# Attention with normalised queries and keys: shifts moved from VectorE and GpSimd to accumulating transfers, and a retuned plan with fewer wide QK matmuls

## The chip, the cores and the metric

The kernel runs on one core of a Trainium2 chip. The metric is the device time of one execution in microseconds (us), a median over several executions. A profile shows a single execution, so its span differs a little from the median, and it leaves out about 2 us at the ends.

Engines in the profile's lines: PE is TensorE's matmul, PEld its weight load, DVE is VectorE, ACT is ScalarE, POOL is GpSimd, SP is SyncE. An engine name with a "q" is that engine's queue of transfer issues.

## The reference

One batch, 32 heads, 2048 positions, head dimension 20, bf16 inputs:

```python
qn = q / (sqrt((q*q).sum(-1, keepdims=True)) + 1e-6)
kn = k / (sqrt((k*k).sum(-1, keepdims=True)) + 1e-6)
logits = einsum('bhqd,bhkd->bhqk', qn, kn) * t[None, :, None, None]
return einsum('bhqk,bhkd->bhqd', softmax(logits), v)
```

The work is dominated by the exponential of 32 x 2048 x 2048 logits, which are 2048 units of 128 rows by 512 columns. In the profile below ScalarE takes 0.453 us for one (650.0 us / 1436 units), so alone it would need 928 us. The kernel shares the exponential between two engines.

## The kernel before

**ScalarE's share.** TensorE writes QK products into PSUM (`psA`), ScalarE takes the exponential two or three units of 512 columns at a time into `p_ring`, and TensorE multiplies these with the values (PV).

**VectorE's share, the "tiles".** A tile is 2048 columns of products in `psD`. VectorE converts it in two instructions of 1024 columns to 16-bit integers, `x*1024*log2(e) + constant`, whose bits are then read as fp16. This is a piecewise linear exponential. To smooth it, TensorE multiplies four versions of the tile with the values: the tile itself and three copies with 256, 512 or 768 added to the integer, each with values scaled down by 2^(-added/1024). The added constants (shifts) are what the change is about:

```python
PHASES = (256, 512, 768)
NX, NE = 4, 3                    # rings: converted tiles, shifted copies
DVE_TILES = [4, 4, 4, 5, ...]    # tiles of each head; 153 in all
KDN = (3, 3, 3, ...)             # tiles of each head whose third shift is GpSimd's
# ... (in add_dgroup: one tile; x is its converted form xt[sx])
for i in range(len(PHASES)):
    dst, war = ss[i][se], t1s + old(f"s{i}", NE)
    if i < 2 or jg < 2 or js[0] - d0[...] >= KDN[...]:
        sh.append([dv(f"s{i}.", lambda e, tk, i=i, dst=dst: e.tensor_scalar(
            dst[:, 0:w], x, float(PHASES[i]), None, ALU.add), 0.533, war)])
        continue
    sh.append([])
    for c in range(0, w // 2, PCH):          # GpSimd, in two halves
        u = add("POOL", f"s{i}.{js[0]}.{c}", lambda e, tk, ...: e.tensor_tensor(...ALU.add), ...)
```

**Preparing a head.** Queries and keys are loaded (`qk_sb`), normalised (`qkn`, on GpSimd), and transposed by a DMA transpose into `qkT`, a ring of three. Ten small transfers, four `qz` and six `kR` (the rotations, below), then copy the transposed rows into four arrangements, which lets four QK matmuls of 32 rows run side by side. SyncE issues them all, in order.

**The plan.** Nothing decides an order on the chip. While the kernel is built, a list scheduler (class `Program`) simulates the engines with an assumed duration for each instruction and an assumed landing time for each transfer (`lat`: 4.5 us for loads of q and k, 3.0 for values, 3.0 for a transpose), and fixes the order of every engine's queue. On the chip each queue runs strictly in that order with semaphore waits. If something lands later than planned, whatever stands behind its waiter in the same queue stops too. (A transfer has landed when its completion is signalled.)

**Wide QK.** The kernel can run a QK matmul over 32, 64 or 128 rows with the same result, the extra rows being zeros. The planner makes matmuls wide where TensorE's load in 3.41 us would otherwise be below a threshold (`LOAD`), so as to hold up its clock.

Of the kernel before, what the change touches and what calls it, by code (L numbers as in the profile page):

```python
# [12 lines left out]
I32 = mybir.dt.int32  # L13
I16 = mybir.dt.int16
# [29 lines left out]
class Program:  # L44
# [5 lines left out]
    SWITCH = 0.25  # L50
# [3 lines left out]
    PASSES = 10  # L54
# [3 lines left out]
    SPARE = 0.0  # L58
    DSL = 0.8
    HOLDA = 9.0  # L60
    HPE = 0.1
    HOLD = {"DVE": 0.0, "PE": HPE}
# [10 lines left out]
    def schedule(self):  # L73


        heavy = set()
        choice = [t for t in self.tasks if t.modes]
        for _ in range(self.PASSES):
            for t in choice:
                tag, t.rows, t.dur, t.work = t.modes[t in heavy]  # L80
                t.name = tag + t.name[2:]
            self.list_schedule()
            pe = [t for t in self.order["PE"] if t.end > self.LIGHT]
            more, i, load = set(), 0, 0.0
            work = [t.work for t in pe]
            for j, t in enumerate(pe):
                while pe[i].end < t.end - self.TICK:
                    load -= work[i]
                    i += 1
                for tier in range(3):  # L90
                    m = j - 1
                    while i and load < self.LOAD and m >= i:
                        u = pe[m]
                        if u.modes and u not in heavy and u not in more and (
                                tier == 2 or u.modes[1][2] == u.dur or tier == 1 and
                                u.modes[1][2] - u.dur <= min(v.start for v in u.users) - u.end - 0.2 - self.SPARE):
                            more.add(u)
                            work[m] += u.modes[1][3] - u.work
                            load += u.modes[1][3] - u.work
                        m -= 1  # L100
                load += work[j]
            if not more:
                break
            heavy |= more
        self.heavy = heavy
        for t in self.tasks:
            if t.trig is not None:
                t.deps.append(t.trig)
        return self.order

    def list_schedule(self):
# [49 lines left out]
        def pool_fill(now):  # L161

            n = 0
            while True:
# [21 lines left out]
                heapq.heappush(events, (t.end, 1, t.seq, t))  # L186
# [135 lines left out]
def bass_standalone__qk_norm__prompt_kernel(  # L322
# [20 lines left out]
    NX = 4  # L343
# [7 lines left out]
    SPREAD = 1.0  # L351
# [5 lines left out]
    DVE_TILES = [4, 4, 4, 5, 5, 5, 5, 5, 4, 5, 5, 5, 5, 5, 4, 5, 5, 5, 5, 5, 4, 5, 5, 5, 5, 5, 4, 5, 5, 5, 5, 5]  # L357
# [7 lines left out]
    KDN = (3, 3, 3, 3, 3, 3, 3, 3, 3, 3, 3, 3, 3, 3, 3, 2, 3, 3, 3, 3, 3, 3, 3, 3, 3, 4, 3, 3, 3, 4, 2, 3)  # L365
# [3 lines left out]
    with ExitStack() as es:  # L369
# [7 lines left out]
        two = sbuf("two", [128, 1], I32)  # L377
        ident = sbuf("ident", [128, 128], BF16)
# [27 lines left out]
        def memset(eng, ap, val, dur, pri):  # L406
            return add(eng, "z", lambda e, tk: e.memset(ap, val), dur, pri=pri)
# [35 lines left out]
        memset("POOL", two[:, :].bitcast(I16), PHASES[2], 0.1, -98)  # L443
# [331 lines left out]
        def add_dgroup(jg):  # L775
# [35 lines left out]
            sh = []  # L811
            for i in range(len(PHASES)):
                dst, war = ss[i][se], t1s + old(f"s{i}", NE)
                if i < 2 or jg < 2 or js[0] - d0[D_tiles[js[0]][0]] >= KDN[D_tiles[js[0]][0] % len(KDN)]:
                    sh.append([dv(f"s{i}.", lambda e, tk, i=i, dst=dst: e.tensor_scalar(  # L815
                        dst[:, 0:w], x, float(PHASES[i]), None, ALU.add), 0.533, war)])
                    continue
                sh.append([])
                for c in range(0, w // 2, PCH):
                    n = min(PCH, w // 2 - c)  # L820
                    u = add("POOL", f"s{i}.{js[0]}.{c}", lambda e, tk, i=i, dst=dst, c=c, n=n: e.tensor_tensor(  # L821
                        dst[:, 2 * c:2 * (c + n)].bitcast(I32), xt[sx][:, 2 * c:2 * (c + n)].bitcast(I32),
                        bass.AP(two, 0, [two[:, :].ap[0], [0, n]]), ALU.add), 0.25 + n * PRATE, war, due + SHP)
                    u.win = 0.02 + n * PRATE
                    sh[-1].append(u)
            dusers["x", jg] = [u for us in sh for u in us]
            for nm, tile, dep, ph in [("x", xt[sx], t1s, None)] + [(f"s{i}", ss[i][se], sh[i], i) for i in range(len(PHASES))]:
                us = dusers.setdefault((nm, jg), [])
                for i, j in enumerate(js):
                    h, rg = D_tiles[j]  # L830
                    p = add("PE", f"pv{nm}{j}", lambda e, tk, h=h, rg=rg, i=i, tile=tile, ph=ph: pv_mm(
                        e, h, lambda g: rg[g],
                        lambda g: tile[:, 2048 * i + 512 * GORD[g]:2048 * i + 512 * GORD[g] + 512].bitcast(FP16), ph),
                        PE_MM, dep + pv_base(h) + (vsc[h] if ph is not None else []), due + 0.2)
                    pv_users[h].append(p)
                    us.append(p)
# [76 lines left out]
```

## Time and profile before

Four executions: median 667.70 us (667.33 to 667.84).

| | before |
|---|---|
| span of the profiled execution | 665.3 us |
| ScalarE busy / VectorE busy | 657.1 (99%) / 654.2 (98%) |
| TensorE / GpSimd busy | 601.3 (90%) / 355.3 (53%) |
| granted TensorE clock | 0.999 |
| DMA | 36.24 MB, queue q1 34.5% of the engines' time |

These are lines of the page of the kernel before: busy times, clock in 40 slices, DMA queue, the chain of waits that ended last by engine, and three groups. A group line has line, engine, operation, tiles and shapes, count, then busy us and mean ns of one, then the engine's idle time just before such instructions and what ended most of it.

```profile
PE 601.3 (90%) x5914; PEld 166.3 (25%) x5959; DVE 654.2 (98%) x927; ACT 657.1 (99%) x584; POOL 355.3 (53%) x364
PEclk9999999999999999999999999999999999999999
q1 hardware_dynamic: 196512, 35.22, 34.5%
ACT 90%; DVE 5%; DMA 1%; SPq 1%; PE 1%; POOL 0%; issue 0%; ACTq 0%
L757 ACT ACTIVATE p_ring<-psA 128x1024 bf16<-128x1024 f32 (+1 forms) x575 | 650.0, 1371 | 2.8 <-PE psA L666 2.7
L803 DVE TENSOR_SCALAR xt<-psD 128x1024 int16<-128x1024 f32 x306 | 371.1, 1213 | 4.4 <-PE psD L666 3.3
L815 DVE TENSOR_SCALAR ss<-xt 128x2048 int16<-128x2048 int16 x365 | 241.8, 683 | 0.9
```

The two exponential engines are both full; in 650 us of exp, ScalarE waited 2.8 us. A quicker kernel therefore needs less work on both. VectorE's shifts, 241.8 us, are the natural thing to give away.

### The profile page before, as it was taken

How to read it: one execution, taken by the hardware profiler on the slowest of the kernel's cores; microseconds unless marked ns; L12 is line 12 of the kernel's file. 1: busy time of each engine (PE TensorE's matmuls, PEld its weight loads, DVE VectorE, ACT ScalarE, POOL GpSimd, SP SyncE). 2: the span in 40 equal slices, each digit the busy share in tenths (PEclk: the TensorE clock that was granted, in tenths of full speed). 3: DMA queues.
4: the chain of work that ended last, by engine and by line, in shares of the span. 5: the costliest groups of instructions: out<-in, count | busy, mean ns of one | idle time of the engine just before them, and what ended most of it. 6: DMA issues, size and time to landing. Idle time of an engine off the chain costs nothing.

```text
span 665.3 us, 14541 instructions
## 1 busy us (share of the span) xinstructions
PE 601.3 (90%) x5914; PEld 166.3 (25%) x5959; DVE 654.2 (98%) x927; ACT 657.1 (99%) x584; POOL 355.3 (53%) x364
## 2 busy tenths in 40 slices
PE   7798989989889999898999999999899989999987
PEld 2222222222222222222222222222222222222221
DVE  8999999999999999999999999999999999999997
ACT  9999999999999999999999999999999999999997
POOL 2346664573655645565365446556466566655622
PEclk9999999999999999999999999999999999999999
DMA  5554434134242442544035142352414415231200
GB/s 64 67 80 76 65 48 78 19 78 54 41 81 21 81 51 45 89 62 75 4 74 62 32 79 28 68 68 44 80 17 91 45 30 81 39 80 11 55 6 11
DMA packets 196723, 36.24 MB, mean 54 GB/s; under 512 B 172592, under 2 KB 196656, under 8 KB 196656
## 3 DMA queue, kind: packets, MB, share of 16 engines
q1 hardware_dynamic: 196512, 35.22, 34.5%
q8 instruction: 47, 0.77, 0.5%
q14 instruction: 20, 0.16, 0.1%
q10 hardware_dynamic: 144, 0.08, 0.1%
HBM read 7.87 MB, written 2.62 MB: 16 GB/s over the span
## 4 chain that ended last, share of the span: by engine, by line
ACT 90%; DVE 5%; DMA 1%; SPq 1%; PE 1%; POOL 0%; issue 0%; ACTq 0%
ACT p_ring L757 89%; DVE xt L803 3%; DVE ss L815 2%; SPq L404 1%; DMA qk_sb<-in_q_dram 1%; DMA qkT<-qkn 0%; ACT qz L450 0%; PE psA L666 0%; PE psD L666 0%; DMA qz<-qkT 0%; POOL qkn L561 0%; POOL ss L821 0%; DVE oT L699 0%; ACT L440 0%; PE psO L686 0%
## 5 line engine op out<-in xcount | busy, mean ns | idle before, releaser
L757 ACT ACTIVATE p_ring<-psA 128x1024 bf16<-128x1024 f32 (+1 forms) x575 | 650.0, 1371 | 2.8 <-PE psA L666 2.7
L803 DVE TENSOR_SCALAR xt<-psD 128x1024 int16<-128x1024 f32 x306 | 371.1, 1213 | 4.4 <-PE psD L666 3.3
L821 POOL TENSOR_TENSOR ss<-xt,two 128x512 int32<-128x512 int32 x188 | 236.0, 1256 | 163.2 <-DVE ss L815 83.4
L666 PE MATMUL psA<-qz,kR 32*128 32x512 bf16 (+2 forms) x1051 | 227.2, 384 | 36.4 <-ACT p_ring L757 27.7
L815 DVE TENSOR_SCALAR ss<-xt 128x2048 int16<-128x2048 int16 x365 | 241.8, 683 | 0.9
L686 PE MATMUL psO<-ss,vph 128*32 128x512 f16 x1836 | 172.9, 385 | 0.1
L686 PE MATMUL psO<-p_ring,vaug 128*32 128x512 bf16 x1436 | 132.9, 384 | 0.1
L666 PE MATMUL psA<-qz,qkT 32*128 32x512 bf16 (+2 forms) x354 | 117.6, 384 | 12.6 <-ACT p_ring L757 10.3
L666 PE MATMUL psD<-qz,kR 64*128 64x512 bf16 (+1 forms) x454 | 120.9, 384 | 7.9 <-DVE xt L803 4.8
L666 PEld LDWEIGHTS psA<-qz,kR 32*128 32x128 bf16 (+2 forms) x1077 | 54.4, 92 | 181.0 <-ACT p_ring L757 176.2
L494 POOL TENSOR_SCALAR vph<-vaug 128x160 f16<-128x160 bf16 (+1 forms) x96 | 40.0, 417 | 80.8 <-DMA vaug<-in_v_dram 39.8
L561 POOL TENSOR_TENSOR qkn<-qk_sb,rs_r 128x640 bf16<-128x640 bf16 x29 | 47.5, 1639 | 37.4 <-DVE ss L815 19.0
L686 PEld LDWEIGHTS psO<-ss,vph 128*32 128x32 f16 x1836 | 44.3, 94 | 81.4 <-issue 56.5
L686 PE MATMUL psO<-xt,vaug 128*32 128x512 f16 x612 | 60.3, 385 | 0.0
L666 PE MATMUL psD<-qz,qkT 64*128 64x512 bf16 (+1 forms) x144 | 54.3, 385 | 1.4 <-DVE xt L803 0.9
L686 PEld LDWEIGHTS psO<-p_ring,vaug 128*32 128x32 bf16 x1436 | 35.7, 94 | 52.4 <-issue 44.1
L666 PEld LDWEIGHTS psD<-qz,kR 64*128 64x128 bf16 (+1 forms) x459 | 29.6, 93 | 68.3 <-DVE xt L803 50.8
L666 PEld LDWEIGHTS psA<-qz,qkT 64*128 64x128 bf16 (+2 forms) x359 | 28.5, 92 | 58.4 <-ACT p_ring L757 55.1
L710 POOL TENSOR_TENSOR o_stage<-oT,rec 128x320 bf16<-128x320 f32 x30 | 29.0, 967 | 18.3 <-DVE ss L815 14.3
L528 DVE TENSOR_REDUCE rs_sum<-sq 128x32 f32<-128x640 bf16 x32 | 25.7, 806 | 0.1
L699 DVE STREAM_TRANSPOSE oT<-psO 128x512 f32<-128x512 f32 x32 | 22.5, 704 | 1.0 <-PE psO L686 1.0
L686 PEld LDWEIGHTS psO<-xt,vaug 128*32 128x32 bf16 x612 | 15.8, 94 | 28.1 <-issue 20.8
(46 smaller groups left out, 87.3 us busy)
## 6 DMA issues: line engine op xcount, KB each, us to landing
kR<-qkT SPq DMA_DIRECT2D x62, 96.0 KB, 2.2
qz<-qkT SPq DMA_DIRECT2D x124, 32.0 KB, 1.8
kR<-qkT SPq DMA_DIRECT2D x62, 64.0 KB, 2.0
qk_sb<-in_k_dram SPq DMA_DIRECT2D x32, 80.0 KB, 2.6
vaug<-in_v_dram SPq DMA_DIRECT2D x32, 80.0 KB, 3.7
qk_sb<-in_q_dram SPq DMA_DIRECT2D x124, 20.0 KB, 2.6
out_dram<-o_stage SPq DMA_DIRECT2D x31, 80.0 KB, 2.2
kR<-qkT SPq DMA_DIRECT2D x62, 32.0 KB, 1.9
```

Source lines behind the costliest of these rows:

```text
L404: return add(eng, name, lambda e, tk: e.dma_start(dst, src), dur, deps, pri, lat=lat, dma=key)
L494: vsc[h] = [add("POOL", f"vs{h}", lambda e, tk, i=i: e.tensor_scalar(vph[bv][:, i, 0:nd, :], vaug[bv][:, R - nd:R, :], 2.0 ** (-PHASES[i] ...
L528: sums.append(dv("sum", lambda e, tk, i=i, sqb=sqb: e.tensor_reduce(rs["sum"][:, 2 * R * i:2 * R * (i + 1)], sqb[:, :, :], AXIS_X, ALU.add ...
L561: u = add("POOL", f"norm{h}", lambda e, tk, x=x, b=b, i=i, j=j: e.tensor_tensor(qkn[b][:, j:j + m, 0:D], x[:, j:j + m, :], bc(rs["r"][:, 2 ...
L666: return eng.matmul(dst, lhsT, mov, tile_position=(p0, 0))
L686: last = eng.matmul(psO[32 * g:32 * g + 32, :], w, rhs_of(g), start=start, stop=False, skip_group_check=True, tile_position=(0, 32 * g))
L699: trO[h] = add("DVE", f"tr{h}", lambda e, tk: e.transpose(oT[:, :, :].rearrange("p r d -> p (r d)"), psO[:, :]), 0.63, [lambda: pv_users[h ...
L710: fin[h] = add("POOL" if pool else "DVE", f"fin{h}", lambda e, tk: e.tensor_tensor(st, src, rb, ALU.mult), TTDUR if pool else 0.40, [rc] + ...
L757: act[w] = add("ACT", f"exp{w}", lambda e, tk: e.activation(p_ring[:, p0 * 512:p0 * 512 + n], psA[:, slot * WAVES[0] * 512:slot * WAVES[0] ...
L803: t1_prev[nchunk[0]] = add("DVE", f"t1.{j}.{k}", lambda e, tk, o=o, slot=slot: e.tensor_scalar(xt[sx][:, o:o + W1], psD[:, slot * W1:slot ...
L815: sh.append([dv(f"s{i}.", lambda e, tk, i=i, dst=dst: e.tensor_scalar(dst[:, 0:w], x, float(PHASES[i]), None, ALU.add), 0.533, war)])
L821: u = add("POOL", f"s{i}.{js[0]}.{c}", lambda e, tk, i=i, dst=dst, c=c, n=n: e.tensor_tensor(dst[:, 2 * c:2 * (c + n)].bitcast(I32), xt[sx ...
```

## The change

**Intent.** For two tiles of most heads, the third shift needs no engine at all: once the plain tile and its other shifts have been used, a transfer that accumulates adds the constant 768 from a constant tile `cst` onto the converted tile in place. GpSimd only issues it. GpSimd's own shifts go from 188 half tiles to 154. The freed time lets VectorE take 158 tiles instead of 153, and ScalarE 1416 exp units instead of 1436. The ring of converted tiles grows from four to six, since a tile now lives longer. The planner is retuned, and drops wide QK where the 3.41 us windows have load to spare.

```diff
-    SWITCH = 0.25
+    SWITCH = 0.1
-    PASSES = 10
+    PASSES = 12
-    SPARE = 0.0
-    DSL = 0.8
-    HOLDA = 9.0
+    SPARE = 0.05
+    DSL = 0.3
+    HOLDA = 0.6
# ... the loop over wide QK: a window's load is now kept for every matmul,
#     and in early passes:
+                    if u in heavy and ... and min(loads[m:hi[m] + 1]) - gain(u) >= self.LOAD + self.MARGIN:
+                        drop.add(u)
+            heavy = heavy - drop | more
# ...
-    NX = 4
+    NX = 6
-    SPREAD = 1.0
+    SPREAD = 0.8
-    DVE_TILES = [4, 4, 4, 5, ...]          # 153
+    DVE_TILES = [4, 4, 5, 4, ...]          # 158
-    KDN = (3, 3, 3, ...)
+    KDN = (1, 2, 4, 3, ...)
+    ADUR, ALAT = 0.95, 6.5                 # planned issue and landing of an accumulation
+    ACCN = (3, 2, 2, 2, 3, ...)            # third shifts by transfer, of each head
+    cst = sbuf("cst", [128, 2048], I16)    # filled with 768
# ...
+                if dep is None:
+                    us = dusers["x", jg]
+                    tile = xt[sx]
+                    dep = [add("POOL", f"acc{js[0]}", lambda e, tk: e.dma_start(x, cst[:, 0:w], accum_op=ALU.add), ADUR,
+                               us + [z_cst], due + 0.1, lat=ALAT, dma=f"A{sx}")]
```

There are 63 such transfers of 512 KB, each in 128 packets of 4 KB.

More of the change, by code (lines that the diff above doesn't have):

```diff
@@ L53 @@
     LOAD = 3500.0
-    PASSES = 10
+    PASSES = 12
+    FIRM = 4
+    MARGIN = 300.0
     PE_REST = 4.2
@@ L57 @@
     OVER = 0.03
-    SPARE = 0.0
-    DSL = 0.8
-    HOLDA = 9.0
+    SPARE = 0.05
+    DSL = 0.3
+    HOLDA = 0.6
     HPE = 0.1
-    HOLD = {"DVE": 0.0, "PE": HPE}
+    HDV = 0.08
+    HOLD = {"DVE": HDV, "PE": HPE}
     def __init__(self):
@@ L77, in schedule @@
         choice = [t for t in self.tasks if t.modes]
-        for _ in range(self.PASSES):
+        for k in range(self.PASSES):
             for t in choice:
@@ L83, in schedule @@
             pe = [t for t in self.order["PE"] if t.end > self.LIGHT]
-            more, i, load = set(), 0, 0.0
-            work = [t.work for t in pe]
+            n = len(pe)
+            gain = lambda u: u.modes[1][3] - u.modes[0][3]
+            lo, loads, i, load = [], [], 0, 0.0
             for j, t in enumerate(pe):
+                load += t.work
                 while pe[i].end < t.end - self.TICK:
-                    load -= work[i]
+                    load -= pe[i].work
                     i += 1
-                for tier in range(3):
+                lo.append(i)
+                loads.append(load)
@@ new lines, in schedule @@
+            hi = [0] * n
+            for j in range(n):
+                hi[lo[j]] = j
+            for j in range(1, n):
+                hi[j] = max(hi[j], hi[j - 1])
+            drop, more = set(), set()
+            if k < self.PASSES - self.FIRM:
+                for m, u in enumerate(pe):
+                    if u in heavy and u.modes[1][2] > u.modes[0][2] + 0.02 and \
+                            min(loads[m:hi[m] + 1]) - gain(u) >= self.LOAD + self.MARGIN:
+                        drop.add(u)
+                        for x in range(m, hi[m] + 1):
+                            loads[x] -= gain(u)
@@ L91, in schedule @@
+            for j, t in enumerate(pe):
+                for tier in range(4):
                     m = j - 1
-                    while i and load < self.LOAD and m >= i:
+                    while lo[j] and loads[j] < self.LOAD and m >= lo[j]:
                         u = pe[m]
-                        if u.modes and u not in heavy and u not in more and (
-                                tier == 2 or u.modes[1][2] == u.dur or tier == 1 and
-                                u.modes[1][2] - u.dur <= min(v.start for v in u.users) - u.end - 0.2 - self.SPARE):
-                            more.add(u)
-                            work[m] += u.modes[1][3] - u.work
-                            load += u.modes[1][3] - u.work
+                        if u.modes and u not in heavy and u not in more:
+                            cost = u.modes[1][2] - u.dur
+                            if tier == 3 or cost <= 0 or tier == 1 and cost <= min(
+                                    v.start for v in u.users) - u.end - 0.2 - self.SPARE or tier == 2 and u.name[2] == "A":
+                                more.add(u)
+                                for x in range(m, hi[m] + 1):
+                                    loads[x] += gain(u)
@@ L100, in schedule @@
                         m -= 1
-                load += work[j]
-            if not more:
+            if not more and not drop:
                 break
-            heavy |= more
+            heavy = heavy - drop | more
         self.heavy = heavy
@@ L185, in pool_fill @@
                 order["POOL"].append(t)
-                heapq.heappush(events, (t.end, 1, t.seq, t))
+                heapq.heappush(events, (free["POOL"], 1, t.seq, t))
                 leave(t, now)
@@ L356, in bass_standalone__qk_norm__prompt_kernel @@
     DLM = 2
-    DVE_TILES = [4, 4, 4, 5, 5, 5, 5, 5, 4, 5, 5, 5, 5, 5, 4, 5, 5, 5, 5, 5, 4, 5, 5, 5, 5, 5, 4, 5, 5, 5, 5, 5]
+    DVE_TILES = [4, 4, 5, 4, 5, 5, 5, 5, 5, 5, 5, 5, 5, 4, 5, 5, 6, 5, 5, 5, 5, 5, 5, 5, 5, 5, 5, 5, 5, 5, 5, 6]
     NDMAX = 6
@@ L364, in bass_standalone__qk_norm__prompt_kernel @@
     NCH = 1
-    KDN = (3, 3, 3, 3, 3, 3, 3, 3, 3, 3, 3, 3, 3, 3, 3, 2, 3, 3, 3, 3, 3, 3, 3, 3, 3, 4, 3, 3, 3, 4, 2, 3)
+    KDN = (1, 2, 4, 3, 4, 2, 3, 2, 5, 3, 4, 2, 3, 5, 5, 2, 3, 2, 3, 2, 5, 2, 2, 4, 4, 2, 4, 5, 5, 2, 3, 2)
+    ADUR, ALAT = 0.95, 6.5
+    PSH = 2
+    ASTEP, AOFF = 2, 0
+    ACCN = (3, 2, 2, 2, 3, 2, 3, 2, 2, 2, 2, 2, 1, 3, 2, 2, 2, 2, 2, 1, 2, 2, 2, 3, 3, 2, 2, 2, 2, 2, 1, 2)
+    NLAST = 1
     PCH, PRATE = 512, 0.00164
@@ L442, in bass_standalone__qk_norm__prompt_kernel @@
         z_one = memset("DVE", ones[:, :], 1.0, 0.2, -99)
-        memset("POOL", two[:, :].bitcast(I16), PHASES[2], 0.1, -98)
+        memset("POOL", two[:, :].bitcast(I16), PHASES[PSH], 0.1, -98)
+        z_cst = memset("POOL", cst[:, :], PHASES[2], 0.3, -70)
         z_id = add("POOL", "id", lambda e, tk: e.affine_select(
@@ L811, in add_dgroup @@
             sh = []
+            h0, n0 = D_tiles[js[0]][0], js[0] - d0[D_tiles[js[0]][0]]
+            nd0 = DVE_TILES[h0]
+            order = [(n * ASTEP + AOFF) % nd0 if math.gcd(ASTEP, nd0) == 1 else n for n in range(nd0)]
+            kind = order.index(n0)
+            by_dma = jg >= 2 and h0 < H - NLAST and kind < ACCN[h0]
+            by_pool = jg >= 2 and not by_dma and kind < ACCN[h0] + KDN[h0]
             for i in range(len(PHASES)):
                 dst, war = ss[i][se], t1s + old(f"s{i}", NE)
-                if i < 2 or jg < 2 or js[0] - d0[D_tiles[js[0]][0]] >= KDN[D_tiles[js[0]][0] % len(KDN)]:
+                if i == 2 and by_dma:
+                    sh.append(None)
+                elif i != PSH or not by_pool:
@@ L815, in add_dgroup @@
                     sh.append([dv(f"s{i}.", lambda e, tk, i=i, dst=dst: e.tensor_scalar(
                         dst[:, 0:w], x, float(PHASES[i]), None, ALU.add), 0.533, war)])
-                    continue
-                sh.append([])
-                for c in range(0, w // 2, PCH):
-                    n = min(PCH, w // 2 - c)
-                    u = add("POOL", f"s{i}.{js[0]}.{c}", lambda e, tk, i=i, dst=dst, c=c, n=n: e.tensor_tensor(
-                        dst[:, 2 * c:2 * (c + n)].bitcast(I32), xt[sx][:, 2 * c:2 * (c + n)].bitcast(I32),
-                        bass.AP(two, 0, [two[:, :].ap[0], [0, n]]), ALU.add), 0.25 + n * PRATE, war, due + SHP)
-                    u.win = 0.02 + n * PRATE
-                    sh[-1].append(u)
@@ L826, in add_dgroup @@
-            dusers["x", jg] = [u for us in sh for u in us]
-            for nm, tile, dep, ph in [("x", xt[sx], t1s, None)] + [(f"s{i}", ss[i][se], sh[i], i) for i in range(len(PHASES))]:
-                us = dusers.setdefault((nm, jg), [])
+                else:
+                    sh.append([])
+                    for c in range(0, w // 2, PCH):
+                        n = min(PCH, w // 2 - c)
+                        u = add("POOL", f"s{i}.{js[0]}.{c}", lambda e, tk, i=i, dst=dst, c=c, n=n: e.tensor_tensor(
+                            dst[:, 2 * c:2 * (c + n)].bitcast(I32), xt[sx][:, 2 * c:2 * (c + n)].bitcast(I32),
+                            bass.AP(two, 0, [two[:, :].ap[0], [0, n]]), ALU.add), 0.25 + n * PRATE, war, due + SHP)
+                        u.win = 0.02 + n * PRATE
+                        sh[-1].append(u)
@@ new lines, in add_dgroup @@
+            dusers["x", jg] = [u for us in sh if us for u in us]
+            parts = [("x", xt[sx], t1s, None)] + [(f"s{i}", ss[i][se], sh[i], i) for i in range(len(PHASES))]
+            for nm, tile, dep, ph in parts:
+                us = dusers.setdefault((nm, jg), [])
+                if dep is None:
[3 more added lines that the diff above has]
+                               us + [z_cst], due + 0.1, lat=ALAT, dma=f"A{sx}")]
```

## The prediction

> **What bounds the kernel now.** Two engines, almost equally. The page's busy times are ScalarE 657.1 us (99%) and VectorE 654.2 us (98%) of a 665.3 us span; TensorE shows 601.3, GpSimd 355.3, and the DMA engines are about 35% busy (queue list). The chain of waits is 90% ScalarE, nearly all of it the exp on line 757. The granted clock is 0.999. In the groups, ScalarE waits for TensorE only 2.8 us in all, VectorE's PSUM conversions (line 803) 4.4 us. So time falls only if ScalarE gets fewer exp units, and VectorE has to find room for them.
>
> **What the change does, in counts of instructions.** VectorE takes 158 tiles of 2048 columns instead of 153, so ScalarE has 1416 exp units of 512 columns instead of 1436. Of each VectorE tile's three shifts, the third leaves VectorE more often: 63 accumulating transfers are new, GpSimd shifts fall from 188 half tiles to 154, VectorE shifts fall from 365 to 334, and VectorE PSUM conversions rise from 306 to 316.
>
> **Costs from the trace.**
> - ScalarE: exp busy 650.0 us / 1436 units = 0.453 us a unit (union; single instructions overlap). 20 fewer units: -9.1 us, to about 641 us of exp.
> - VectorE: +10 conversions x 1.213 us = +12.1; -31 shifts x 0.66 us (241.8/365) = -20.5. Net -8.4, to about 645.8 us. This saving barely more than pays for the five tiles, as intended: both engines stay balanced.
> - GpSimd: -34 x 1.26 = -43 us, +63 descriptor generations. Estimate about 1 us each, so it stays near 55% busy.
> - DMA: 63 x 512 KB. The Trainium skill, "DMA: Bandwidth & Descriptors", section Anatomy of one DMA, fits a software-generated transfer at 2.0 us + bytes/436 GB/s: 3.2 us for a copy; accumulating also reads the destination, so I estimate 4 to 8 us from issue to landing. No trace here shows it yet. DMA share rises from 35% to perhaps 50-60%.
> - TensorE: same number of PV matmuls a tile; some 128- and 64-row QK matmuls become narrower, which removes a few us from an engine with slack.
>
> **On the critical path.** All of ScalarE's 9.1 us, because ScalarE's exp runs nearly without gaps. The 17.6 us of the measured time outside exp (first exp at 8.4 us, two ragged stretches before 55 us, tail) should stay. 667.6 - 9.1 = 658.5. VectorE gives the same floor: 645.8 + 11.1 idle + 2.3 outside the span = 659.2. Two engines both at 98% may add about a microsecond of waits.
>
> **Prediction: 658.9 us (-1.3%), 80% range 655.5 to 664.** Faster by over 2%: 6%; within 2%: 90%; slower by over 2%: 4%.
>
> **What would show each step right or wrong.** Groups: line-757 exp busy near 641 us with idle still under 5 us; VectorE busy 644-648; mean shift still 0.66-0.70 us; accumulating transfers landing in 4-8 us; TensorE waiting for them rarely (PV waiting on DMA below 5 us in total); clock still at least 0.99.
>
> **What would make it wrong.** (a) The Trainium skill, "SBUF — State Buffer", Who interferes with whom, says that GpSimd and VectorE's two-port modes exclude each other, and that descriptor generation is starved by them. If a descriptor generation instead holds VectorE's shifts up (today 0.68 us against 0.60 for undisturbed ones in the chain), 63 x 0.5 us would cost some of the gain. (b) Transfers landing in over 12 us would stall the six-tile ring and the output accumulation at each head's end. (c) Fewer wide QK matmuls could let the clock fall below 0.99, putting TensorE on the chain. (d) Looser gaps at the start or the end, worth 1-3 us either way.

## More of the kernel before

Heads from the third on are prepared in pairs.

```python
trn[h] = add("SP", f"trn{h}", lambda e, tk: e.dma_start_transpose(qkT[bt]..., qkn[b]...),
             1.3, norm[h] + war, due + 0.1, lat=3.0, dma=f"T{bt}")
rot[h] = [dma("SP", f"qz{h}", qz[bt][...], qkT[bt][...], [trn[h], ...], due + 0.15, ...) for g in range(4)]
# ... and six  dma("SP", f"rot{h}", kR[bt][...], qkT[bt][...], [trn[h]], due + 0.2, ...)
```

The view of the tile `qkT` in the kernel before ends with how long its transposes and the transfers that read it took from issue to landing:

```profile
DMA to landing us min/median/max: 1.8/2.0/4.8
```

## The result, and the profile after

The changed kernel took 692.37 us (median of 4, 687.60 to 695.92) against 667.70 us. A ratio in this document is the mean time of one kernel's fast runs over that of the other's of the same rounds, so it is not quite the ratio of the quoted medians. Here it is 1.0366, 95% interval 1.0298 to 1.0433: **slower by 3.7%**. The results are correct. Executions over 1.5% slower than the fastest of the same kernel are left out of the means.

These are the lines of the page after that answer to those above, and the new ones: the issue of the accumulations, their queue, and the PV matmuls that wait for them.

```profile
PE 600.7 (87%) x6019; PEld 164.8 (24%) x6019; DVE 655.5 (95%) x906; ACT 652.0 (94%) x576; POOL 365.6 (53%) x394
PEclk9998999999999999897999999999999989999999
q1 hardware_dynamic: 196512, 35.22, 33.7%
q0 software_dynamic: 9072, 33.03, 26.6%
DVE 47%; ACT 21%; PE 11%; DMA 9%; SPq 8%; issue 2%; POOL 1%; DVEq 0%; POOLq 0%
L785 ACT ACTIVATE p_ring<-psA 128x1024 bf16<-128x1024 f32 (+1 forms) x567 | 644.6, 1341 | 33.7 <-PE psA L694 30.6
L831 DVE TENSOR_SCALAR xt<-psD 128x1024 int16<-128x1024 f32 x316 | 383.5, 1214 | 26.9 <-PE psD L694 22.6
L851 DVE TENSOR_SCALAR ss<-xt 128x2048 int16<-128x2048 int16 x334 | 226.8, 694 | 0.3
L869 POOL DMA_DIRECT2D xt<-cst x63 | 61.7, 980 | 51.7 <-PE psO L714 30.4
L714 PE MATMUL psO<-xt,vph 128*32 128x512 f16 x252 | 25.7, 399 | 8.0 <-DMA xt<-cst 8.0
xt<-cst POOLq DMA_DIRECT2D x63, 512.0 KB, 5.4
```

The instructions did what was planned. What changed is idle time. Exp is 5.4 us less busy, but its idle time grew by 30.9 us (2.8 to 33.7). These sum to 25.5 us, nearly the whole 26.7 us by which the span grew (665.3 to 692.0). ScalarE and VectorE now wait for TensorE, yet TensorE's busy time is unchanged and its share fell. So TensorE waits too. PV waits for accumulations account for 8.0 us of it in the line above, or 9.6 us as the weight loads show them in the view of the tile `cst`; these are the same waits seen on two queues, not a sum.

A table of two stages of the same length shows how local this is. First the kernel before; columns are the stretch, its length, the busy us (and instructions) of each engine, the granted clock, the mean DMA share and GB/s:

```profile
core 0: us, PE busy (x) PEld busy (x) DVE busy (x) ACT busy (x) POOL busy (x), PEclk, DMA share, GB/s
260.00:300.00 40.00, 35.22 (x360) 9.71 (x362) 38.44 (x53) 40.00 (x37) 23.73 (x25) 1.00 0.53 80
300.00:340.00 40.00, 37.23 (x364) 9.94 (x364) 39.91 (x57) 40.00 (x36) 20.75 (x20) 1.00 0.28 43
```

The same stretches after, and four short ones inside them (same columns):

```profile
260.00:300.00 40.00, 33.51 (x332) 8.79 (x333) 35.26 (x47) 35.17 (x32) 18.28 (x21) 0.91 0.70 79
300.00:340.00 40.00, 29.37 (x286) 7.67 (x282) 30.48 (x48) 31.60 (x28) 19.51 (x19) 0.87 0.65 113
280.60:284.00 3.40, 0.04 (x2) 0.00 (x0) 0.97 (x2) 1.36 (x2) 0.00 (x0) 0.82 1.65 43
284.00:289.60 5.60, 5.57 (x36) 0.95 (x36) 3.29 (x4) 3.38 (x3) 3.02 (x6) 0.50 0.36 48
319.00:325.70 6.70, 0.23 (x8) 0.00 (x0) 0.99 (x3) 1.60 (x2) 1.63 (x2) 0.60 0.76 162
325.70:330.60 4.90, 4.79 (x30) 0.93 (x31) 2.87 (x4) 2.47 (x2) 0.96 (x3) 0.50 0.75 94
```

TensorE stands still for 3.4 us at 280.6 and for 6.6 us at 319. After each stall it works at half clock for about 5 us, and in these stretches both exponential engines are busy only 50 to 60% of the time. (A DMA share above 1 must be packets that overlap on one engine and are each counted.) Within the span, the clock records show 37.5 us at half clock after, against 2.0 before, all of those in the tail. Each of the six half-clock stretches after follows a stall of TensorE, of 1.1 to 6.6 us.

What do these stalls wait for? From the chain of waits of the kernel after, in order of time: start us, duration us, what. Pieces called "issue" of under 0.1 us are left out throughout.

```profile
271.76 12.23 DMA xt<-cst
284.03 0.62 PE psO L714 x4
...
303.75 1.66 POOL qkn L589
305.43 9.98 DMA qkT<-qkn
315.43 0.59 SPq L431
316.06 1.57 SPq L431
317.67 0.59 SPq L431
318.31 0.59 SPq L431
...
320.85 1.45 SPq L431
322.34 0.81 SPq L431
323.20 2.52 DMA kR<-qkT
325.81 0.61 PE psD L694 x2
```

The first stall waits for an accumulation that took 12.23 us to land. The second starts with a transpose that took 9.98 us from issue to landing; behind it SyncE issues ten transfers at some 0.6 us each, and TensorE waits for the last `kR`. The view of `qkT` after ends with this line, against a maximum of 4.8 before:

```profile
DMA to landing us min/median/max: 1.8/2.6/12.3
```

The packet records show what the two late ones share. The columns are the start and end in us of a transfer's first and last packet on the DMA engines, not counting issue and completion:

```
transpose 273.40 to 282.87 (9.47 us)   accumulation 273.93 to 283.16 (9.23 us)
transpose 306.63 to 314.78 (8.15 us)   accumulation 307.18 to 314.70 (7.52 us)
```

A transpose with nothing beside it takes 1.4 us by the same measure, and an accumulation about 3.3 us. Both pairs started within 0.6 us of each other, and then held each other up to the end. Overlap alone is not enough: eleven more transposes of this run overlapped an accumulation that had started some 2.5 us or more before them, or that started 1.3 us or more after them, and these took 1.36 to 1.98 us.

Of the 33.7 us of exp idle time, 13.2 lie between 273 and 332 us, in and behind these two pairs. The rest belongs to other stalls, and they differ: before the one of 46.5 to 51.8 us, two accumulations (43.1 to 50.5) ran beside head 2's rotation transfers, and six `kR` issues took 6.58 us instead of 3.78; around 120 us a load of values landed in 7.56 us where the plan had 3.0, the scaling of the values behind it held up GpSimd's queue for 6.0 us, and TensorE then waited 1.1 us for the accumulation that this queue issued next.

### The profile page after: what moved, and what is told of

It reads as the page before. It is cut to its first block, busy times and chain, and to the rows that moved or that the text cites. A ratio compares the mean times of both kernels' runs of the same rounds, so it can differ in the third digit from the quotient of the medians.

```text
span 692.0 us, 14735 instructions
## 1 busy us (share of the span) xinstructions
PE 600.7 (87%) x6019; PEld 164.8 (24%) x6019; DVE 655.5 (95%) x906; ACT 652.0 (94%) x576; POOL 365.6 (53%) x394
## 3 DMA queue, kind: packets, MB, share of 16 engines
q1 hardware_dynamic: 196512, 35.22, 33.7%
q0 software_dynamic: 9072, 33.03, 26.6%
## 4 chain that ended last, share of the span: by engine, by line
DVE 47%; ACT 21%; PE 11%; DMA 9%; SPq 8%; issue 2%; POOL 1%; DVEq 0%; POOLq 0%
DVE xt L831 27%; ACT p_ring L785 21%; DVE ss L851 15%; SPq L431 8%; PE psO L714 5%; PE psA L694 3%; DMA xt<-cst 3%; DMA vaug<-in_v_dram 2%; PE psD L694 2%; DVE oT L727 2%; DMA qkT<-qkn 1%; DVE rs_sum L556 1%; DVE sq L554 1%; DMA kR<-qkT 1%; DMA qk_sb<-in_q_dram 1%
## 5 line engine op out<-in xcount | busy, mean ns | idle before, releaser
L785 ACT ACTIVATE p_ring<-psA 128x1024 bf16<-128x1024 f32 (+1 forms) x567 | 644.6, 1341 | 33.7 <-PE psA L694 30.6
L831 DVE TENSOR_SCALAR xt<-psD 128x1024 int16<-128x1024 f32 x316 | 383.5, 1214 | 26.9 <-PE psD L694 22.6
L857 POOL TENSOR_TENSOR ss<-xt,two 128x512 int32<-128x512 int32 x154 | 190.6, 1238 | 129.6 <-DVE ss L851 58.3
L851 DVE TENSOR_SCALAR ss<-xt 128x2048 int16<-128x2048 int16 x334 | 226.8, 694 | 0.3
L714 PE MATMUL psO<-ss,vph 128*32 128x512 f16 x1644 | 155.4, 392 | 3.5 <-POOL ss L857 2.7
L694 PE MATMUL psD<-qz,kR 64*128 64x512 bf16 (+1 forms) x474 | 124.9, 392 | 32.9 <-DVE xt L831 17.1
L694 PE MATMUL psA<-qz,qkT 64*128 64x512 bf16 (+2 forms) x354 | 119.0, 390 | 10.8 <-ACT p_ring L785 9.5
L522 POOL TENSOR_SCALAR vph<-vaug 128x160 f16<-128x160 bf16 (+2 forms) x96 | 38.5, 401 | 101.2 <-DMA vaug<-in_v_dram 77.6
L869 POOL DMA_DIRECT2D xt<-cst x63 | 61.7, 980 | 51.7 <-PE psO L714 30.4
L694 PE MATMUL psD<-qz,qkT 64*128 64x512 bf16 (+1 forms) x158 | 60.7, 393 | 3.1 <-DVE xt L831 2.5
L589 POOL TENSOR_TENSOR qkn<-qk_sb,rs_r 128x640 bf16<-128x640 bf16 x29 | 45.4, 1573 | 21.2 <-DVE ss L851 6.9
L714 PE MATMUL psO<-xt,vph 128*32 128x512 f16 x252 | 25.7, 399 | 8.0 <-DMA xt<-cst 8.0
```

What stands on the lines that cost most here:

```text
L522: vsc[h] = [add("POOL", f"vs{h}", lambda e, tk, i=i: e.tensor_scalar(vph[bv][:, i, 0:nd, :], vaug[bv][:, R - nd:R, :], 2.0 ** (-PHASES[i] ...
L589: u = add("POOL", f"norm{h}", lambda e, tk, x=x, b=b, i=i, j=j: e.tensor_tensor(qkn[b][:, j:j + m, 0:D], x[:, j:j + m, :], bc(rs["r"][:, 2 ...
L694: return eng.matmul(dst, lhsT, mov, tile_position=(p0, 0))
L714: last = eng.matmul(psO[32 * g:32 * g + 32, :], w, rhs_of(g), start=start, stop=False, skip_group_check=True, tile_position=(0, 32 * g))
L785: act[w] = add("ACT", f"exp{w}", lambda e, tk: e.activation(p_ring[:, p0 * 512:p0 * 512 + n], psA[:, slot * WAVES[0] * 512:slot * WAVES[0] ...
L831: t1_prev[nchunk[0]] = add("DVE", f"t1.{j}.{k}", lambda e, tk, o=o, slot=slot: e.tensor_scalar(xt[sx][:, o:o + W1], psD[:, slot * W1:slot ...
```

## The experiments

All ratios are to the kernel before in the same rounds. The clock is the mean granted TensorE clock, and "exp idle" ScalarE's idle time before exp instructions, both of the profiled execution; before has 0.999 and 2.8 us, after 0.973 and 33.7 us.

| run | what | median us | ratio | clock | exp idle us |
|---|---|---|---|---|---|
| e1 | after, no accumulations, tiles as before | 667.43 | 0.9987 | 1.000 | 1.2 |
| e2 | after, old wide-QK rule | 721.84 | 1.0804 | 0.965 | 48.4 |
| e3 | after, transfers of 1/8 the bytes (wrong result) | 660.38 | 0.9884 | 0.995 | 4.4 |
| e4 | after, copies that don't accumulate (wrong result) | 665.86 | 0.9980 | 0.997 | 7.3 |
| e5 | after, mutual waits of transposes and accumulations | 716.08 | 1.0710 | 0.955 | 54.7 |
| e7 | after, longer planned landing times | 676.03 | 1.0142 | 0.989 | 16.1 |
| e8 | e5 and e7 together | 681.14 | 1.0201 | 0.982 | 18.5 |
| e9 | e7, no accumulation in the first 50 us | 667.05 | 0.9986 | 0.997 | 5.3 |
| e10 | e9, transposes wait for earlier accumulations | 678.80 | 1.0159 | 0.979 | 17.1 |
| e11 | before, 60 unread transfers of 512 KB | 717.37 | 1.0741 | 0.972 | 45.4 |
| e12 | before, 60 unread transfers of 8 KB | 671.96 | 1.0070 | 1.000 | 5.2 |
| e13 | e7, replanned (64 transfers) | 675.89 | 1.0119 | 0.993 | 12.3 |
| e14 | before, 17 unread transfers away from transposes | 675.01 | 1.0118 | 0.997 | 9.6 |
| e15 | before, 17 unread transfers at transposes | 719.75 | 1.0772 | 0.971 | 48.2 |
| e16 | before, 60 unread transfers of 256 KB | 676.08 | 1.0134 | 0.999 | 8.2 |
| e17 | accumulations planned apart from transposes | 664.47 | 0.9950 | 0.994 | 7.1 |

The first theory was that the transfers' traffic makes other transfers land late. Its rivals were that fewer wide QK matmuls lower the clock, and that the retuned plan is worse in itself.

### e1: the change without its transfers

```diff
-    DVE_TILES = [4, 4, 5, 4, ...]
-    KDN = (1, 2, 4, 3, ...)
-    ACCN = (3, 2, 2, 2, ...)
+    DVE_TILES = [4, 4, 4, 5, ...]    # those of before
+    KDN = (3, 3, 3, 3, ...)          # those of before
+    ACCN = (0,) * 32
```

> The retuned planner and the narrower QK stay, the accumulating transfers go (none for any head; tiles and GpSimd shares of the kernel before). Theory A (the transfers' traffic on the DMA engines makes planned landings late): back to 664-671 us, granted clock 0.99 or more, ScalarE idle before exp under 5 us. Rival B (fewer wide QK matmuls let the clock fall) or rival C (the retuned plan is itself worse): 680 us or more, clock below 0.985.

Measured: 667.43 us (666.32 to 667.77), ratio 0.9987 (0.9970 to 1.0004), clock 1.000, exp idle 1.2 us. With the new planner and its narrower QK (99 matmuls of 128 rows, where before has 198 and after 88), the kernel is as quick as before. Neither the retuning nor narrower QK costs anything by itself. The loss needs the transfers, or the tiles that come with them.

### e2: the change with the old wide-QK rule

```diff
-    PASSES = 12
-    SPARE = 0.05
+    PASSES = 10
+    SPARE = 0.0
# ... and the whole loop over `heavy` as in the kernel before
```

> The changed kernel with the kernel before's rule for choosing wide QK matmuls; everything else stays, transfers too. Theory A: still 684-697 us with clock drops that follow DMA stalls. Rival B: 657-668 us, clock 0.99 or more.

Measured: 721.84 us, ratio 1.0804, clock 0.965, with 330 matmuls of 128 rows. More wide QK did not restore the clock; the kernel became 30 us slower still. This refutes the rival of the narrow QK, but it is also a miss, since no theory expected so large a loss. TensorE was busy 639.9 us instead of 600.7. That it then has less room to recover after a stall is likely but was only argued.

### e3 and e4: the same program with less traffic

```diff
-    e.dma_start(x, cst[:, 0:w], accum_op=ALU.add)
+    e.dma_start(x[:, 0:256], cst[:, 0:256], accum_op=ALU.add)     # e3
+    e.dma_start(x, cst[:, 0:w])                                   # e4
```

Both give a wrong result; every instruction and every wait stays where it was.

> The same program instruction by instruction, but each accumulating transfer covers 256 of the 2048 columns, an eighth of the bytes (result wrong on purpose; same waits, same issue work on GpSimd). Theory A: 656-665 us, clock 0.99 or more, transposes land again in about 3 us, so that the gain of 9 us appears. Rival C (order on GpSimd's queue, thin leads in the plan) and rival D (descriptor generation on GpSimd against VectorE): 680 us or more.

> The same program, same bytes written, but plain copies in place of accumulation (result wrong on purpose). If the accumulation's extra read of the destination is what slows the engines: landing falls from 5.4 to 3-4 us, time to 658-670 us. If the bytes written and the issue alone do it: 684-697 us as the changed kernel.

Measured: e3 660.38 us (659.28 to 661.38), ratio 0.9884 (0.9866 to 0.9903). The page of e3 has these lines for its queue, the chain by engine, exp and shifts:

```profile
q0 software_dynamic: 9072, 4.13, 5.6%
ACT 59%; DVE 34%; PE 4%; issue 1%; DMA 1%; SPq 0%; DVEq 0%
L785 ACT ACTIVATE p_ring<-psA 128x1024 bf16<-128x1024 f32 (+1 forms) x567 | 641.3, 1380 | 4.4 <-PE psA L694 4.1
L851 DVE TENSOR_SCALAR ss<-xt 128x2048 int16<-128x2048 int16 x334 | 226.5, 693 | 0.3
```

With 63 issues and 4.13 MB instead of 33.03 MB, the predicted gain is there: exp is busy 641.3 us, idle 4.4. The bytes, not the issues, the waits or the plan, cost 32 us (692.37 - 660.38). e3 does not tell whether they do so through other transfers or through their own late landing, since the short ones also land sooner (2.9 us, median). In e4 the same bytes without accumulation gave 665.86 us (664.25 to 669.0), landing in 3.7 us (median) instead of 5.4. A plain copy's 4 KB packet took 162 ns (median), an accumulating one 340 ns. So of the 32 us, moving the bytes accounts for about 5.5 (665.86 - 660.38) and accumulating them for the other 26.5. Plain copies slow transposes too: the longest in e4, 5.13 us on the engines, met a copy that started 0.46 us after it.

### e5, e7 and e8: keep the two apart with waits, or plan for later landings

```diff
# e5, after the plan is made; the plan itself is unchanged
+        for a in self.tasks:
+            for t in self.tasks:
+                if a.name[:3] == "acc" and t.name[:3] == "trn" and t.dma and abs(a.start - t.start) < 9.0:
+                    if a.start < t.start:
+                        t.deps.append(a)
+                    else:
+                        a.deps.append(t)
# e7: planned landing times, from the fourth head on
-    lat=4.5 (loads of q, k), 3.0 (values), 3.0 (transpose)
+    lat=7.5,                 8.0,          6.0
# e8: both
```

> The changed kernel with waits added so that a transpose and an accumulating transfer planned within 9 us of each other are never in flight together (the later in the plan waits for the earlier to land). Theory A1 (the loss comes mainly from the two collisions in which a transpose took 8 and 9.5 us and an accumulation 12): 668-680 us, no transpose above 3 us. Theory A2 (late landings of every kind, rotations, V loads, and queues that serve in order): 683-697 us.

> The changed kernel, planned with longer landing times for loads (7.5 and 8 us in place of 4.5 and 3) and transposes (6 in place of 3); transfers unchanged. If the plan's thin margins for those landings are what turns slow DMA into stalls (A2): 665-680 us and fewer gaps of ScalarE. If the accumulations' own lateness and collisions decide (A1): 684-697 us.

> Both: the waits of e5_fence and the longer planned landings. If A1 and A2 each carry part: 660-672 us, clock 0.99, the best correct version with accumulation so far. If neither: 684-697 us, and the accumulation's own rate is what remains.

Measured: e5 716.08 us, e7 676.03 (675.85 to 681.11), e8 681.14 (ratio 1.0201). In e5 the waits did what they should to the transfers: no transpose took over 2.74 us on the engines and no accumulation more than 7.9 us to land. Still the kernel lost 24 us more, for a wait in an in-order queue stops everything behind it, normalisations and GpSimd's shifts among them (one PV waited 4.24 us for a GpSimd shift). The theory's "keep them apart and the loss goes" fell in this form. Planning for later landings, without a wait, won 16 us of the 25; two stalls were left, at 52 and 316 us, both for `kR`. In e7 four transposes took 4.16 to 6.72 us on the engines, and only the last of them was followed by a stall, so with room in the plan a slow transpose need not cost anything. e8 kept every transpose under 2.9 us and was still 5 us slower than e7: its waits cost more than they saved.

### e9 and e10: no transfers at the start; a one-way wait

```diff
# e9, from e7
-    ACCN = (3, 2, 2, ...)
-    KDN = (1, 2, 4, ...)
+    ACCN = (2, 0, 2, ...)
+    KDN = (1, 4, 4, ...)
# e10, from e9
+                if a.name[:3] == "acc" and t.name[:3] == "trn" and t.dma and 0.0 <= t.start - a.start < 7.0:
+                    t.deps.append(a)
```

> e7_longer_plan (longer planned landings) with no accumulating transfer in the first 50 us, so that the rotations of the third head have the DMA engines to themselves. If that early stall (5 us of e7 and as long at half clock after it) is the traffic's: the stall near 50 us goes and the time falls from 676 to 664-671 us. If the stall belongs to the plan of the start: no change from 676.

> e9_late_start plus one-way waits: a transpose planned within 7 us after an accumulating transfer waits until that has landed (no wait on GpSimd's queue, unlike e5_fence and e8). If the collision that held up e7 near 305 us is all that is left: 657-665 us, clock 0.995 or more, faster than the kernel before by about 1%. If waits in SP's queue cost more than collisions: slower than e9_late_start.

Measured: e9 666.05 us, the median of four fast runs (665.64 to 667.96), ratio 0.9986 (0.9966 to 1.0006). Two more runs, of 676.67 and 676.72, are slow and do not enter. The profile is of a fast run, so what the slow ones met is not known. e10, at 678.80 us, shows again that a wait in SyncE's queue costs more than it saves: VectorE now waits for late loads, 2.71 us once and 2.05 another time.

### e11, e12 and e16: the traffic alone, in the kernel before

```diff
# the plan of before is made, then 60 transfers are put into GpSimd's queue, 10.2 us apart
+        for i in range(60):
+            u = Task("POOL", f"acc{i}", lambda e, tk, i=i: e.dma_start(
+                dummy[i % 2][:, 0:N], kx[:, 0:N].bitcast(I16),
+                **({"accum_op": ALU.add} if i > 1 else {})), 0.95, ...)
+            u.start = 36.0 + 10.2 * i
# N = 2048 columns in e11, 32 in e12, 1024 in e16
```

No engine reads what these transfers write. GpSimd only waits, before an issue, for the transfer two places earlier, some 20 us before, which used the same scratch tile. The results stay correct and the four other engines keep their orders.

> The kernel before, its plan untouched, with 60 transfers of 512 KB (58 accumulating) into two scratch tiles that nobody reads, one each 10.2 us. If the traffic alone slows a plan (theory A without the changed plan): 675-695 us, clock below 0.99, stalls on rotations or V loads. If it takes traffic and the changed plan's thinner margins together: 667-673 us. Result correct.

> The control of e11: the same 60 issues on GpSimd, 64 bytes a partition. Theory A: 667-670 us, as the kernel before. If issuing on GpSimd (descriptor generation, its queue's order) is what costs: as e11.

> e11_traffic_in_before with 1024 of the 2048 columns a transfer, half the bytes. If the loss goes with bytes: about 690-695 us. If short transfers slip past the margins of the plan: under 682 us.

Measured: e11 717.37 us (ratio 1.0741), e12 671.96 (1.0070), e16 676.08 (1.0134). So 60 issues cost 4.7 us, and the bytes of e11 another 45 us. So such a loss does not need TensorE to wait for accumulated data, since here no such data is waited for. Half the bytes cost only 9 us in all where the full bytes cost 50: the loss is far from proportional to bytes. e11's chain by engine shows where it goes:

```profile
DVE 49%; SPq 23%; DMA 10%; PE 6%; POOL 5%; issue 4%; ACT 2%; ACTq 0%; POOLq 0%
```

SyncE's queue of issues is on the chain for 23%, and a transpose's landing took up to 10.6 us. Three of its 60 transfers started 0.5 to 0.8 us after a transpose and made a pair of transposes take 8.0 to 10.0 us; 23.0 of its 45.4 us of exp idle time lie in and behind these meetings (354 to 398 and 489 to 580 us). The other stalls follow none. In e16, too, three transfers met a pair at such a place, but the pairs took only 5.4 to 6.5 us.

### e14 and e15: meeting a transpose or not

```diff
# as e11, but 17 transfers, at the places that the plan of before offers
+        trn_at = [v.start for v in prog.tasks if v.name[:3] == "trn" and v.dma]
# e14: a gap in GpSimd's queue with no transpose planned in the 6 us before or the 8 us after it
+            if ... and not any(-8.0 < u.end - x < 6.0 for x in trn_at):
# e15: a gap close to a transpose
+            if ... and any(-1.5 < u.end - x < 2.5 for x in trn_at):
```

> The kernel before with 17 unread transfers of 512 KB, each at least 6 us away from every planned transpose. If meeting a transpose is what hurts (A1): 667-671 us, transposes land in about 3 us. If load on the engines hurts anywhere (A2): 17/60 of e11's loss of 50 us, 677-685 us.

> The same 17 transfers, each issued at the same time as a transpose. A1: at least 10 us slower than e14, 680-700 us, many transposes of 6 us and more. A2: within 4 us of e14.

Measured: e14 675.01 us (672.5 to 679.12), e15 718.16 (three fast runs, 716.47 to 721.34; a fourth, of 729.37, is slow). The number and size of transfers are the same; only their places differ. From the page of e14, the queue of the transfers, the chain by engine and exp, and then the last line of the view of `qkT`:

```profile
q0 software_dynamic: 2448, 8.91, 6.7%
DVE 68%; ACT 12%; SPq 12%; PE 3%; DMA 2%; issue 2%; POOL 1%; ACTq 0%
L758 ACT ACTIVATE p_ring<-psA 128x1024 bf16<-128x1024 f32 (+1 forms) x575 | 652.4, 1329 | 9.6 <-PE psA L667 8.8
```

```profile
DMA to landing us min/median/max: 1.8/2.0/5.4
```

And the same of e15:

```profile
q0 software_dynamic: 2448, 8.91, 7.7%
DVE 46%; ACT 16%; SPq 13%; DMA 11%; PE 8%; POOL 3%; issue 3%; ACTq 0%; POOLq 0%
L758 ACT ACTIVATE p_ring<-psA 128x1024 bf16<-128x1024 f32 (+1 forms) x575 | 655.3, 1299 | 48.2 <-PE psA L667 47.2
```

```profile
DMA to landing us min/median/max: 1.8/2.0/11.5
```

A transfer kept clear costs about 0.5 us (8 us for 17), one sent at a transpose about 3.0 us (51 us for 17). Seventeen that meet a transpose cost as much as sixty spread evenly. In e15 six pairs of transposes, of which one by itself takes 1.4 us, were 9.9 to 10.8 us a pair on the engines, and in all six the accumulation's first packet came 0.5 to 0.7 us after the transposes' first. A place beside a transpose is also close to its rotations and to the loads of the next heads, which these runs don't separate.

### e13 and e17: a new plan without and with the rule

Both start from e7, take no transfers in the first 50 us and have the counts of tiles, GpSimd shifts and transfers searched again by the planner. e13 also plans 7.5 us for an accumulation. Only e17 has the rule, which keeps the planner from issuing an accumulation within 3 us after a transpose or a normalisation. It takes another ready instruction of GpSimd instead, so no wait is added.

```diff
# e17, in the list scheduler
+                if t.name[:4] == "norm":
+                    clear[0] = max(clear[0], t.end + 3.0)
# ...
-                    x = min(r for r in ready[e] if not r[2].win)
+                    cand = [r for r in ready[e] if not r[2].win and not (
+                        r[2].name[:3] == "acc" and now < clear[0])]
+                    if not cand:
+                        continue
+                    x = min(cand)
# ...
+                if e == "SP" and t.name[:3] == "trn":
+                    clear[0] = max(clear[0], now + 3.0)
```

> e9_late_start taken further: planned landing of accumulations 1 us longer as well, and tile counts, transfer counts and GpSimd shares searched again under these landings (157 tiles instead of 158, no transfer before 50 us). Thin margins (A2): 658-666 us, faster than the kernel before by 0.3 to 1.4%, clock 0.995 or more, and a smaller spread than e9. If stalls come from the traffic whatever the plan: 668-685 us.

> The planner itself is taught not to issue an accumulating transfer in the 3 us after a transpose or its normalisation (no wait is added), with the longer planned landings of e7, no transfer in the first 50 us, and tile and transfer counts searched again (59 or fewer transfers). If meeting a transpose is the main cost: no transpose near 8 us, 657-664 us, faster than the kernel before by 0.5 to 1.5% and the best correct version. If loaded engines still make landings late often enough: 666-676 us as e9 and e13.

Measured: e13 675.89 us (671.88 to 677.95), a miss. Four of its transposes still met an accumulation and took 6.75 to 8.91 us. e17 took 664.47 us (664.0 to 665.14, five runs), ratio 0.9950 (0.9937 to 0.9964), with the correct result. From the page of e17:

```profile
q0 software_dynamic: 7776, 28.32, 23.2%
ACT 84%; DVE 5%; PE 4%; SPq 3%; DMA 3%; issue 1%; POOL 0%
L797 ACT ACTIVATE p_ring<-psA 128x1024 bf16<-128x1024 f32 (+1 forms) x568 | 642.7, 1385 | 7.1 <-PE psA L706 7.0
```

ScalarE holds the chain again (84%), exp idle is 7.1 us, and no transpose takes over 3.3 us on the engines although 28.32 of the 33.03 MB are still moved. One stall is left, at 483.7 us, where VectorE waited 4.71 us for a load of q. e17 is the quickest correct kernel here, 28 us below the changed kernel and 0.5% below before. It has 157 tiles and 54 transfers, so the rule is not its only difference from e13 (64 transfers). By e14's 0.5 us each, ten transfers fewer would be worth 5 of the 11 us between them, which is an estimate. And e9, without the rule, already reached the time of before in its fast runs, with three transposes of 4.24 to 4.77 us. So e17 agrees with the explanation but does not prove it; how much the rule itself won is not shown.

## Why the prediction was wrong

Point by point, as the prediction put it:

- **"20 fewer units: -9.1 us, to about 641 us of exp."** Right in kind and size: 641.3 us in e3, 644.6 in the kernel after with its stalls.
- **VectorE "about 645.8 us".** Slightly low. Without the traffic (e3) it was busy 650.2. The 31 shifts saved 15.3 us in e3 (241.8 to 226.5) rather than 20.5, in part because the remaining ones took 693 instead of 683 ns. This does not decide anything: e3 is at 660.4 us with it.
- **"63 descriptor generations. Estimate about 1 us each."** Right: 980 ns.
- **"4 to 8 us from issue to landing."** Right for the median, 5.4 us, and wrong for the tail, up to 12.2.
- **"DMA share rises from 35% to perhaps 50-60%."** Right (33.7% and 26.6%). The step that failed is the next one, on the critical path: the prediction drew nothing from this traffic. "ScalarE's exp runs nearly without gaps" was carried over from the kernel before to the kernel after, as "All of ScalarE's 9.1 us"; the idle time before exp, expected "under 5 us", was 33.7. The prediction priced an accumulation by how long its own reader waits. It had no term for what the transfer does to the others in flight.
- **What stood in its place.** The traffic delays other transfers. Where an accumulation starts within about 0.8 us after a transpose, both slow down: from 1.4 to 8.15 and 9.47 us on the engines (after), and to 8 to 11 us for a pair of transposes (e11, e15). The transpose feeds the QK of the next head through ten issues in SyncE's in-order queue, under a plan that had given it 3.0 us. TensorE's queue stops, then both exponential engines. e3 (bytes away, loss away) and e11 (bytes alone, loss there) show that the traffic is the cause. e14 against e15 (same bytes, 8 us or 51 us) shows that the place of a transfer beside a head's preparation decides what it costs, in the plan of before. How much of the changed kernel's 25 us the two meetings cost is not isolated: 13.2 of its 33.7 us of exp idle time lie in and behind them. The rest belongs to other late transfers: rotations, loads, and accumulations issued late behind a load.
- **"TensorE waiting for them rarely (PV waiting on DMA below 5 us in total)".** Wrong, 8.0 to 9.6 us. Three of the six half-clock stretches (at 125.8, 282.8 and 555.8 us) follow such a wait, so it has a part, but e11 loses twice as much without a reader.
- **"clock still at least 0.99".** Wrong, 0.973. The half-clock stretches follow the stalls, and the risk named for it, fewer wide matmuls, is refuted by e1 (clock 1.000 with half as many) and by e2. The Trainium skill, "TensorE: Matmul & The Clock Gate", section What's actually happening, says that an idle window of some 3.4 us halves the clock and that a busy window restores it. The trace agrees in part: the stalls of 3.4 and 6.6 us are followed by 5 us at 0.50, and every such stretch lasts one, two or three times 3.41 us. But the window need not be wholly idle: in the 3.41 us before five of the six drops TensorE was still busy for 1.26 to 1.92 us, and once the only gap of over 0.5 us in it was one of 1.1 us (at 124.5). The half clock should make a stall dearer than its length, but no run isolates how much of the 25 us it adds.
- **Risk (a), descriptor generation.** The Trainium skill, "SBUF — State Buffer", section Who interferes with whom, says that GpSimd and VectorE's two-port instructions block each other, and that the making of descriptors suffers from it. Here shifts became 11 ns longer (683 to 694) and 60 issues alone cost 4.7 us (e12), real but a tenth of e11's loss; that the ports are the reason is not shown. Risk (b) named transfers "in over 12 us" but expected them to stall the ring of tiles. One accumulation did take 12.2 us, and it held up PV for 3.4 us; the longest stall, 6.6 us, came from a late transpose.

Three things stay open: what in the DMA engines makes a transpose and an accumulation slow each other, how the changed kernel's loss divides among its stalls, and why e2 is so much slower.

## What to carry to other kernels

Before work is moved from an engine to a transfer, ask what else is in flight when it runs, and how much lateness the queues behind those transfers can take, for idle bandwidth is no answer to that. The effect can be measured in the old kernel with transfers that nobody reads, at chosen places. Where two kinds of transfer hold each other up, try a plan with later landings (e7 won 16 us) or one in which they don't meet (e17); a wait put into an in-order queue cost more here than it saved (e5, e10).

## What the Trainium skill lacked or had wrong

- "DMA: Bandwidth & Descriptors", section Rules for kernel authors, says "A transpose next to ordinary DMAs needs nothing". In context this is about corrupted data, and the results here were indeed correct. Nothing there or on another page says that a transpose and an accumulating transfer which start together slow each other: 1.4 us became 8.15 and 9.47 us for the transpose in the kernel after, and the accumulation went from about 3.3 to 7.5 and 9.2 us. Seventeen such transfers cost 51 us at transposes (e15) and 8 us away from them (e14).
- The same page gives no rate for an accumulating transfer. Within SBUF, 512 KB landed in 5.4 us (median), a plain copy in 3.7 us (e4); a 4 KB packet took 340 and 162 ns. The page's fit, section Anatomy of one DMA, gives an estimate of 3.2 us for a copy of that size, half a microsecond below e4.
- "SBUF — State Buffer", section Who interferes with whom, gives no size for what issuing costs VectorE in a mixed kernel: 60 small transfers cost the kernel 4.7 us (e12), and VectorE's shifts were 11 ns of 683 longer beside 63 issues.
- "TensorE: Matmul & The Clock Gate" does not say how little work makes a window count as idle. Here the clock fell after windows of 3.41 us in which TensorE was busy for up to 1.92 us.
